# The last product transposed, and for the second pair of batches computed by seven block products instead of eight

## Chip, cores and metric

The kernel runs on one core of a Trainium2 chip. The metric is the device time of one execution in microseconds; the time before is the median of three runs.

## The reference

Attention of tokens against a state gives 4 x (512 + 32) = 2176 rows of 512 numbers; a softplus layer (512 to 2048 to 512) and a gated SiLU layer (512 to 1536 to 512) follow. Cut to what matters here:

```python
x = np.concatenate([xread, sread], axis=2)      # 4 batches, 512 tokens + 32 state rows, 512
h = x @ w_in
g = np.maximum(h, 0.0) + np.log1p(np.exp(-np.abs(h)))
x = g @ w_out                                   # layer one
g = x @ w_gate
silu = g * (1.0 / (1.0 + np.exp(-g)))
val = x @ w_val
out = silu * val @ w_out                        # layer two, its last product
```

## The kernel before

Every float32 operand is split into a high and a low part (fp32r), and every product takes three matmuls: high·high, low·high, high·low (`mm3`, L85 to L89). The split is a copy on ACT (`split_act`, L574) and a subtraction on POOL (`low`, L92).

Layer one (to 350 us) isn't touched. Layer two runs in 24 steps n: pair p = n // 12 of two batches, slice f = n % 12 of 128 hidden columns. In a step gate and value for both batches of the pair are one 2x2 block product, done in Strassen's way by seven products P1 to P7 of six matmuls each (`quad_mm`, `PARTS`), 128x128 stationary and 128x512 moving. P1, P6, P7 and P4 add up in one PSUM bank, px, and between them ACT copies it to cA (L891), cB (L904) and cC (L912); P5 and P3 add up in pz, P2 stands in py. DVE adds py to cA (L901), pz to cC (L918), multiplies px by cA (L922), which is the activation of the pair's first batch (cA), and adds pz to cB (L927). ACT's Silu of cB (L875) and POOL's product with cC (L876) give that of the second batch (cC); the latter, and the split of both, fall into the beginning of the next step.

The last product (`out_mm`) runs two steps later for an f-pair q of two slices: in step n that of slices n-2-n%2 and the next, batch n%2. For each of four row groups r a 128x128 slice of the activation is stationary and w2 (512 columns) moves, six matmuls into a bank po, which DVE adds to oacc in SBUF (L595; for q = 0 a copy, L592). In the rows of the trace w is w2, and h and l are the high and low part of an activation. Two groups stand after P6 and two after P7 in each step (`outs`), 24 matmuls; those of the last f-pair stand at the very end, and at q = 5 each group is stored (L598). The 32 state rows of all batches go through three small products (`state_1` to `state_3`) in steps 0 to 13.

The order of the work is written out by hand: the Python order of the calls is the order on every engine. Small pieces of other work (splitting the second layer's weights into DRAM, the split of the second pair's inputs) are hung on named points of a step by `at2` and run by `run2`. SP issues all DMAs in program order: `load_gw` (L230, four of 512 KB for step n+2 at the end of step n), `load_w2` (L234, two of 512 KB in odd steps), stores.

Of the kernel before, what the change touches and what calls it, by code (L numbers as in the profile page):

```python
# [8 lines left out]
F32 = mybir.dt.float32  # L9
F32R = mybir.dt.float32r  # L10
# [6 lines left out]
P = 128  # L17
# [20 lines left out]
def attention_moe_moe2_kernel(  # L38
# [540 lines left out]
    out_v = out.rearrange("(b t) d -> b t d", b=B)

    def out_mm(n, j, r, store=True):

        p, q = n // NF, n % NF // 2
        b = 2 * p + j
        ps = bank("y", f"po{n}_{j}_{r}")
        t = slice(r * P, (r + 1) * P)
        for f in range(2):
            mm3(ps, [x[:, t] for x in act[n + f, j]], [w2[n + f][:, i, :] for i in range(2)], f == 0, f == 1)
        if q == 0:
            if r % 2 == 0:  # L590
                oacc[b, r // 2] = slot([P, 2, DM], F32, "yacc", f"oacc{b}_{r // 2}")
            nc.vector.tensor_copy(oacc[b, r // 2][:, r % 2, :], ps)  # L592
            return
        v = oacc[b, r // 2][:, r % 2, :]
        nc.vector.tensor_tensor(out=v, in0=ps, in1=v, op=ALU.add)  # L595
# [35 lines left out]
    def state_3(q):  # L631
        ps = bank("y", f"pt3{q}")
        for f in range(2):
            t = slice(f * P, (f + 1) * P)
            mm3(ps, [x[:, t] for x in gs[q]], [w2[2 * q + f][:, i, :] for i in range(2)], f == 0, f == 1)
        if q == 0:
            os_[0] = const.tile([P, DM], F32, tag="yo", name="os_")
            nc.vector.tensor_copy(os_[0], ps)
        else:
            nc.vector.tensor_tensor(out=os_[0], in0=ps, in1=os_[0], op=ALU.add)  # L640
        if q == NQ - 1:
            for b in range(B):
# [8 lines left out]
    with tc.manual_schedule(engines={ENG.PE}):  # L651
# [220 lines left out]
        pending = []  # L872

        def value_times_gate(n, c):
            nc.scalar.activation(c["B"], c["B"], AF.Silu)  # L875
            nc.gpsimd.tensor_tensor(out=c["C"], in0=c["C"], in1=c["B"], op=ALU.mult)  # L876
            yield
            split_act(n, 1, c["C"])

        with tc.manual_schedule(engines={ENG.DVE, ENG.SP, ENG.Activation, ENG.Pool}):  # L880
            run2(-1, "load0")
            run2(-1, "load1")
            for n in range(NS2):
                run2(n, "load0")
                run2(n, "load1")
                c = {}
                for k in "ABC":
                    c[k] = work.tile([P, 512], F32, tag=k, name=f"c{k}{n}")
                x = quad_bank(f"px{n}")
                quad_mm(x, n, "P1", True)  # L890
# [32 lines left out]
                split_act(n, 0, c["A"])  # L923
# [4 lines left out]
                pending.append(value_times_gate(n, c))  # L928
# [49 lines left out]
```

## Time and profile before

| what | value |
|---|---|
| median of 3 runs | 744.88 us (744.71 to 745.37) |
| span of the profiled execution | 742.8 us |
| PE busy | 717.5 us, 97%, 3640 matmuls |
| DVE, POOL, ACT busy | 442.5, 389.6, 316.0 us |
| DMA moved | 143.78 MB, mean 194 GB/s |

The profile gives the profiled execution's own time by its span alone, 742.8 us, from the first to the last recorded work; the runs' times include what lies around it. Busy time is that of one engine; waits and their releasers are inferred from semaphores.

### The profile page before, as it was taken

To read this page: it belongs to the slowest core of one execution; us is meant where nothing else is said; L and a number is where in the kernel's file an instruction comes from. 1 tells how busy PE (TensorE), PEld (TensorE's weight loads), DVE (VectorE), ACT (ScalarE), POOL (GpSimd) and SP (SyncE) were. 2 spreads that over 40 slices of the span, in tenths; PEclk is the share of its full clock that TensorE was granted. 3 is DMA by queue.
4 is the path that set the end of the run, shared out by engine and by line. 5 is a ranking of instruction groups with operands and counts; after the bars stand their busy time and mean duration, and the time that the engine had idled before them with its cause. 6 is when DMAs were issued, how large, how long until landed. Compare 5 with 4: busy or idle time off the path is not lost.

```text
span 742.8 us, 10024 instructions
## 1 busy us (share of the span) xinstructions
PE 717.5 (97%) x3640; PEld 567.3 (76%) x3640; DVE 442.5 (60%) x605; ACT 316.0 (43%) x586; POOL 389.6 (52%) x352
## 2 busy tenths in 40 slices
PE   4699999999999999999999999999999999999997
PEld 1367767786777777788788888888888888888885
DVE  5984559877767867458676656554554333333334
ACT  3767445644545545444544444442542222222221
POOL 2467537787648765834576767765452222222222
PEclk9999999999999999999999999999999999999999
DMA  9930215654544545470579979778355943447302
GB/s 339 408 118 0 86 58 170 197 201 169 160 152 168 192 124 169 160 265 1 197 286 356 348 258 340 286 284 307 114 198 189 315 162 142 170 133 262 143 1 113
DMA packets 51072, 143.78 MB, mean 194 GB/s; under 512 B 5712, under 2 KB 18000, under 8 KB 51024
## 3 DMA queue, kind: packets, MB, share of 16 engines
q1 hardware_dynamic: 51024, 143.15, 54.5%
q8 instruction: 28, 0.46, 0.2%
q14 instruction: 20, 0.16, 0.1%
HBM read 107.22 MB, written 35.91 MB: 193 GB/s over the span
## 4 chain that ended last, share of the span: by engine, by line
PE 86%; DVE 2%; POOL 2%; issue 1%; ACT 1%; DVEq 0%; POOLq 0%; ACTq 0%
PE py L89 25%; PE px L89 18%; PE po L89 18%; PE ph L89 9%; PE pz L89 9%; PE pt L89 3%; PE ps L505 2%; PE pm L374 2%; PE ps L89 1%; POOL sums_gv L193 1%; POOL gv L92 0%; POOL l L92 0%; DVE t_wo L136 0%; DVE m L92 0%; DVE t_win L143 0%
## 5 line engine op out<-in xcount | busy, mean ns | idle before, releaser
L89 PE MATMUL py<-h,wo 128*128 128x512 f32 x512 | 158.8, 391 | 1.5 <-POOL wo L92 1.3
L92 POOL TENSOR_TENSOR l<-C,h 128x512 fp32r<-128x512 f32 x64 | 91.2, 1430 | 86.5 <-ACT C L407 68.9
L89 PE MATMUL po<-w,h 128*128 128x512 f32 x384 | 126.2, 391 | 0.0
L89 PEld LDWEIGHTS py<-h,wo 128*128 128x128 f32 x512 | 95.9, 188 | 23.0 <-POOL wo L92 2.0
L89 PE MATMUL ph<-aT,m 128*128 128x512 f32 x384 | 101.3, 399 | 1.6 <-DVE m L92 1.6
L89 PE MATMUL py<-l,wo 128*128 128x512 f32 x256 | 99.9, 390 | 0.0
L89 PEld LDWEIGHTS ph<-aT,m 128*128 128x128 f32 x384 | 70.8, 188 | 25.5 <-issue 6.1
L404 ACT ACTIVATE h<-ph 128x512 fp32r<-128x512 f32 x64 | 38.2, 597 | 120.6 <-PE py L89 116.7
L595 DVE TENSOR_TENSOR oacc<-po,oacc 128x512 f32<-128x512 f32 x80 | 54.8, 690 | 54.9 <-PE po L89 54.3
L89 PEld LDWEIGHTS po<-w,h 128*128 128x128 f32 x384 | 72.1, 188 | 14.8
L92 POOL TENSOR_TENSOR l<-cC,h 128x512 fp32r<-128x512 f32 x24 | 31.5, 1313 | 97.0 <-ACT h L574 83.1
L89 PE MATMUL po<-w,l 128*128 128x512 f32 x192 | 74.8, 390 | 0.5 <-POOL l L92 0.5
L92 POOL TENSOR_TENSOR l<-cA,h 128x512 fp32r<-128x512 f32 x24 | 34.5, 1438 | 77.6 <-ACT h L574 77.6
L89 PE MATMUL px<-T_0s,gw 128*128 128x512 f32 x216 | 60.9, 390 | 1.4 <-ACT cC L912 1.4
L89 PE MATMUL px<-T_1s,gw 128*128 128x512 f32 x216 | 60.7, 389 | 0.0
L89 PEld LDWEIGHTS py<-l,wo 128*128 128x128 f32 x256 | 48.1, 188 | 10.5 <-POOL l L92 0.3
L574 ACT ACTIVATE h<-cA 128x512 fp32r<-128x512 f32 x24 | 15.2, 633 | 91.9 <-DVE cA L922 91.9
L89 PEld LDWEIGHTS px<-T_0s,gw 128*128 128x128 f32 x216 | 40.3, 188 | 10.3 <-ACT cC L912 2.2
L89 PEld LDWEIGHTS px<-T_1s,gw 128*128 128x128 f32 x216 | 40.5, 188 | 8.5
L89 PEld LDWEIGHTS po<-w,l 128*128 128x128 f32 x192 | 36.1, 188 | 8.2 <-POOL l L92 1.0
L901 DVE TENSOR_TENSOR cA<-py,cA 128x512 f32<-128x512 f32 x24 | 16.5, 687 | 42.6 <-PE py L89 36.9
L92 POOL TENSOR_TENSOR split_gv<-sums_gv,split_gv 128x512 fp32r<-128x512 f32 x24 | 33.1, 1379 | 15.2 <-ACT split_gv L197 14.3
(148 smaller groups left out, 1321.1 us busy)
## 6 DMA issues: line engine op xcount, KB each, us to landing
gw<-gv_d SPq DMA_DIRECT2D x96, 512.0 KB, 6.7
gv_d<-gv SPq DMA_DIRECT2D x24, 512.0 KB, 3.6
gv_d<-split_gv SPq DMA_DIRECT2D x24, 512.0 KB, 3.3
w<-w_d SPq DMA_DIRECT2D x24, 512.0 KB, 8.4
raw_win<-in_moe_w_in_dram SPq DMA_DIRECT2D x16, 512.0 KB, 7.2
raw_wo<-in_moe_w_out_dram SPq DMA_DIRECT2D x16, 512.0 KB, 4.0
raw_gv<-in_moe_w_gate_dram SPq DMA_DIRECT2D x48, 128.0 KB, 3.8
raw_gv<-in_moe_w_val_dram SPq DMA_DIRECT2D x48, 128.0 KB, 3.5
```

Of the source, the lines that this page charges most:

```text
L89: nc.tensor.matmul(o, a[s], b[t], start=first and i == 0, stop=last and i == 2, **k)
L92: eng.tensor_tensor(out=o, in0=whole, in1=high.bitcast(F32), op=ALU.subtract)
L193: nc.gpsimd.tensor_tensor(out=o, in0=x, in1=y, op=op)
L374: nc.tensor.matmul(ps[k * NS:(k + 1) * NS, :], st[q, k, b, :], win[c, k].t[q, :], start=True, stop=True)
L404: nc.scalar.activation(self.h, self.ps, AF.Softplus)
L505: nc.tensor.matmul(ps, sw[:, kt, :], win[c, kt].t, start=kt == 0, stop=kt == KT - 1)
L574: nc.scalar.activation(h, src, AF.Copy)
L595: nc.vector.tensor_tensor(out=v, in0=ps, in1=v, op=ALU.add)
L901: nc.vector.tensor_tensor(out=c["A"], in0=y, in1=c["A"], op=ALU.add)
```

## The change

1. The last product is transposed: a 128x128 slice of w2 is stationary and the activation's 512 tokens move. The token part of the output is kept as [batch, column, token] and turned on the host; the state rows go to a second output. In a group the matmuls now read high, high, low of the activation, where they read high, low, high.
2. For the second pair, f-pairs q = 0 to 4 (steps 14 to 23), the last product of both batches and both slices is a 2x2 block product by seven products of six matmuls (`out_part`) instead of eight groups: parts P1, P2, P5 in the even step, P6, P3, P7, P4 in the odd one. It needs four sums of w2 (`OutSums`, made in steps 10, 12, 13, 14 and 16, kept in DRAM, loaded back by `load_w2s`), four sums of activations (`total`, on DVE) and seven splits instead of four. P1, P6, P7 and P4 use one pair of banks after another, P5 and P3 another.
3. In steps 0 and 1 the order P1, P5, P2, P6, state rows, P7, P4, P3 becomes P1, P5, P6, P2, P7, state rows, P4, P3.
4. In odd steps the out part P4 stands between the products P4 and P3 of the step.

```diff
+    class OutSums:
+        def __init__(self, q):
...
+                t = slot([P, 2, 512], F32R, "made", f"w2r{q}_{f}")
+                nc.sync.dma_start(out=t.bitcast(F32), in_=w2_d[2 * q + f])
+        def whole(self):
...
+                nc.vector.tensor_tensor(out=t, in0=r[:, 0].bitcast(F32), in1=r[:, 1].bitcast(F32), op=ALU.add)
+        def sums(self):
+            (a11, a21), (a12, a22) = ((t[:, :256], t[:, 256:]) for t in self.t)
...
+                nc.gpsimd.tensor_tensor(out=o, in0=x, in1=y, op=op)
+        def high(self):
...
+                nc.scalar.activation(o[:, 0, :], self.s[k], AF.Copy)
+        def low(self):
...
+                low(nc.gpsimd, o[:, 1, :], self.s[k], o[:, 0, :])
+                nc.sync.dma_start(out=w2s_d[self.q][:, k], in_=o.bitcast(F32))
+    def load_w2s(q):
+        for k in range(2):
+            w2s[q, k] = slot([P, 2, 512], F32R, "w2s", f"w2s{q}_{k}")
+            nc.sync.dma_start(out=w2s[q, k].bitcast(F32), in_=w2s_d[q][:, k])
...
-            mm3(ps, [x[:, t] for x in act[n + f, j]], [w2[n + f][:, i, :] for i in range(2)], f == 0, f == 1)
+            mm3(ps, [w2[n + f][:, i, dt * P:(dt + 1) * P] for i in range(2)], act[n + f, j], f == 0, f == 1)
...
+    OUTS = {
+        "P1": ("f0", 0, "B11"), "P2": ("f1", 0, "B21"), "P3": ("s", 3, "B22"), "P4": ("f1", 1, "T4"),
+        "P5": ("s", 0, "T1"), "P6": ("s", 1, "T2"), "P7": ("s", 2, "T3"),
+    }
+    def out_part(n, part):
...
+        keep, opens = ("x", part == "P1") if part in ("P1", "P6", "P7", "P4") else ("z", part in ("P2", "P5"))
...
+            ps = opx[keep, i]
...
+            mm3(ps, [w[:, l, c] for l in range(2)], act[n, t], opens, True, skip_group_check=True)
+            out_add(b + j, 2 * m + i, ps, first)
...
+        SLOTS2 = ((("P1",), ("P2",), ("P5",)), (("P6",), ("P3", "P7"), ("P4",)))
+        for q, n in enumerate((10, 12, 13, 14, 16)):
+            at2(n - 1, "load1", lambda q=q, job=job: job.update(s=OutSums(q)))
+            for kind, name in (("conv0", "whole"), ("conv1", "sums"), ("conv2", "high"), ("conv2", "low")):
...
+                def first():
+                    total(c["B"], c["C"], c["A"], ALU.subtract)
+                    split_act((n, "T1"), c["B"])
...
+                def second():
+                    total(b12, b22, b12, ALU.subtract)
+                    total(b11, b12, b11, ALU.add)
+                    split_act((n - 1, "T2"), b11)
+                    split_act((n - 1, "B22"), b22)
+                def third():
+                    total(b21, b21, b11, ALU.subtract)
+                    split_act((n - 1, "T3"), b12)
+                after(n + 1, 1, second)
+                after(n + 1, 2, third)
+                after(n + 2, 0, lambda: split_act((n - 1, "T4"), b21))
...
                 if n < 2:
+                    quad_mm(x, n, "P6", False)
+                    nc.scalar.activation(c["B"], x, AF.Copy)
+                    quad_mm(y, n, "P2", True)
...
+                    quad_mm(x, n, "P7", False)
+                    nc.scalar.activation(c["C"], x, AF.Copy)
+                    nc.scalar.activation(c["A"], c["A"], AF.Silu)
...
+                    nc.vector.tensor_tensor(out=c["C"], in0=z, in1=c["C"], op=ALU.add)
                     run2(n, "state")
...
-                outs(n, 2)
+                parts(n, 1) if n >= NF + 2 else outs(n, 2)
                 quad_mm(x, n, "P4", False)
...
+                if n >= NF + 2:
+                    parts(n, 2)
...
+                if n % 2 and NF - 1 <= n < NS2 - 3:
+                    load_w2s((n + 1) % NF // 2)
```

On PE, step 0 before, from P2 to P4. Every product has two rows of three matmuls, one for each half of the contraction; B21 is the operand of P2, T2 of P6, T3 of P7 and T4 of P4, and pt holds the state rows:

```order
L89 MATMUL py0_3408<-B21_0_0s_3090,gw0_0_0_3227 128x512 x3
L89 MATMUL py0_3408<-B21_0_1s_3122,gw0_1_0_3229 128x512 x3
L89 MATMUL px0_3393<-T2_0_0s_3265,gw0_0_1_3231 128x512 x3
L89 MATMUL px0_3393<-T2_0_1s_3331,gw0_1_1_3233 128x512 x3
L89 MATMUL pt10_3429<-gw0_0_0_3227,yT_3297 128x256 x3
L89 MATMUL pt10_3429<-gw0_1_0_3229,yT_3297 128x256 x3
L89 MATMUL pt10_3429<-gw0_0_0_3227,yT_3297 128x256 x3
L89 MATMUL pt10_3429<-gw0_1_0_3229,yT_3297 128x256 x3
L89 MATMUL px0_3393<-T3_0_0s_3219,gw0_0_1_3231 128x512 x3
L89 MATMUL px0_3393<-T3_0_1s_3311,gw0_1_1_3233 128x512 x3
L89 MATMUL px0_3393<-T4_0_0s_3309,gw0_0_0_3227 128x512 x3
L89 MATMUL px0_3393<-T4_0_1s_3348,gw0_1_0_3229 128x512 x3
```

And after the change:

```order
L90 MATMUL px0_3393<-T2_0_0s_3265,gw0_0_1_3231 128x512 x3
L90 MATMUL px0_3393<-T2_0_1s_3331,gw0_1_1_3233 128x512 x3
L90 MATMUL py0_3408<-B21_0_0s_3090,gw0_0_0_3227 128x512 x3
L90 MATMUL py0_3408<-B21_0_1s_3122,gw0_1_0_3229 128x512 x3
L90 MATMUL px0_3393<-T3_0_0s_3219,gw0_0_1_3231 128x512 x3
L90 MATMUL px0_3393<-T3_0_1s_3311,gw0_1_1_3233 128x512 x3
L90 MATMUL pt10_3437<-gw0_0_0_3227,yT_3297 128x256 x3
L90 MATMUL pt10_3437<-gw0_1_0_3229,yT_3297 128x256 x3
L90 MATMUL pt10_3437<-gw0_0_0_3227,yT_3297 128x256 x3
L90 MATMUL pt10_3437<-gw0_1_0_3229,yT_3297 128x256 x3
L90 MATMUL px0_3393<-T4_0_0s_3309,gw0_0_0_3227 128x512 x3
L90 MATMUL px0_3393<-T4_0_1s_3348,gw0_1_0_3229 128x512 x3
```

P6 stands before P2, and the four rows of the state (twelve matmuls) have moved from before P7 to between P7 and P4.

On PE, step 17 before, the last eight matmuls of the out product, then P4 and P3 of the step (po14_1_2 and po14_1_3 are row groups 2 and 3 of batch 1; w is w2, h and l the activation's parts):

```order
L89 MATMUL po14_1_2_5881<-w215_5489,l15_1_5771 128x512
L89 MATMUL po14_1_2_5881<-w215_5489,h15_1_5770 128x512
L89 MATMUL po14_1_3_5889<-w214_5487,h14_1_5659 128x512
L89 MATMUL po14_1_3_5889<-w214_5487,l14_1_5660 128x512
L89 MATMUL po14_1_3_5889<-w214_5487,h14_1_5659 128x512
L89 MATMUL po14_1_3_5889<-w215_5489,h15_1_5770 128x512
L89 MATMUL po14_1_3_5889<-w215_5489,l15_1_5771 128x512
L89 MATMUL po14_1_3_5889<-w215_5489,h15_1_5770 128x512
L89 MATMUL px17_5820<-T4_1_0s_5218,gw17_0_0_5699 128x512 x3
L89 MATMUL px17_5820<-T4_1_1s_5221,gw17_1_0_5701 128x512 x3
L89 MATMUL pz17_5830<-B22_1_0s_5231,gw17_0_1_5703 128x512 x3
L89 MATMUL pz17_5830<-B22_1_1s_5234,gw17_1_1_5705 128x512 x3
```

After the change, step 17 from the out part P7 on (poP1_14_0 and poP1_14_1 are the pair of banks that P1 opened in step 16; w2s are loaded sums):

```order
L90 MATMUL poP1_14_0_5874<-h14_T3_5949,w2s1_1_5571 128x512 x2
L90 MATMUL poP1_14_0_5874<-l14_T3_5950,w2s1_1_5571 128x512
L90 MATMUL poP1_14_1_5879<-h14_T3_5949,w2s1_1_5571 128x512 x2
L90 MATMUL poP1_14_1_5879<-l14_T3_5950,w2s1_1_5571 128x512
L90 MATMUL px17_5971<-T4_1_0s_5245,gw17_0_0_5818 128x512 x3
L90 MATMUL px17_5971<-T4_1_1s_5248,gw17_1_0_5820 128x512 x3
L90 MATMUL poP1_14_0_5874<-h14_T4_5979,w215_5567 128x512 x2
L90 MATMUL poP1_14_0_5874<-l14_T4_5980,w215_5567 128x512
L90 MATMUL poP1_14_1_5879<-h14_T4_5979,w215_5567 128x512 x2
L90 MATMUL poP1_14_1_5879<-l14_T4_5980,w215_5567 128x512
L90 MATMUL pz17_5985<-B22_1_0s_5258,gw17_0_1_5822 128x512 x3
L90 MATMUL pz17_5985<-B22_1_1s_5261,gw17_1_1_5824 128x512 x3
```

The groups of six into one bank have become parts of two groups of three, which go on adding in banks that DVE has read before; T4's part stands behind the step's own P4. Step 17 keeps 24 matmuls of this product, the even step 16 has 18.

On SP, from the gw loads at the end of step 13, before:

```order
L230 DMA gw15_1_1_5485<-gv3_d_2015 128x1024
L234 DMA w214_5487<-w22_d_1824 128x1024
L234 DMA w215_5489<-w23_d_2184 128x1024
L230 DMA gw16_0_0_5591<-gv4_d_2222 128x1024
L230 DMA gw16_1_0_5593<-gv4_d_2222 128x1024
L230 DMA gw16_0_1_5595<-gv4_d_2222 128x1024
```

And after:

```order
L233 DMA gw15_1_1_5563<-gv3_d_2015 128x1024
L237 DMA w214_5565<-w22_d_1824 128x1024
L237 DMA w215_5567<-w23_d_2184 128x1024
L281 DMA w2s1_0_5569<-w2s1_d_5370 128x1024
L281 DMA w2s1_1_5571<-w2s1_d_5370 128x1024
L276 DMA w2s3_d_5652<-w2o3_0_5648 128x1024
L276 DMA w2s3_d_5652<-w2o3_1_5649 128x1024
L233 DMA gw16_0_0_5701<-gv4_d_2222 128x1024
L233 DMA gw16_1_0_5703<-gv4_d_2222 128x1024
L233 DMA gw16_0_1_5705<-gv4_d_2222 128x1024
L233 DMA gw16_1_1_5707<-gv4_d_2222 128x1024
```

Behind the loads of w2 stand two loads of sums and two stores of new sums, and gw16 comes after them.

## Rows read from the trace of the kernel before

**Rows 1.** Page, part 1: busy time and share of the span of each engine

```profile
PE 717.5 (97%) x3640; PEld 567.3 (76%) x3640; DVE 442.5 (60%) x605; ACT 316.0 (43%) x586; POOL 389.6 (52%) x352
```

**Rows 2.** Page, part 4: the chain that ended last, by engine

```profile
PE 86%; DVE 2%; POOL 2%; issue 1%; ACT 1%; DVEq 0%; POOLq 0%; ACTq 0%
```

**Rows 3.** Windows, one step: length, busy PE PEld DVE ACT POOL, clock, DMA share, GB/s

```profile
591.00:606.00 15.00, 15.00 (x68) 12.43 (x67) 5.54 (x8) 3.98 (x7) 3.87 (x3) 1.00 0.44 139
```

**Rows 4.** Timeline of PE in steps 13 and 14: start, us, what

```profile
566.38 0.39 PE L89 MATMUL po<-w,h 128*128 128x512 f32 x1
...
569.10 0.39 PE L89 MATMUL px<-T_0s,gw 128*128 128x512 f32 x1
...
577.26 0.84 PE L89 MATMUL px<-B_0s,gw 128*128 128x512 f32 x3
```

**Rows 5.** Waits of PE from 340 us on: us in total, times, longest

```profile
PE px L89 <- ACT cC L912: 1.4, 2, 0.7
PE po L89 <- POOL l L92: 0.5, 1, 0.5
```

**Rows 6.** Timeline of PE in steps 0 and 1

```profile
349.67 0.84 PE L89 MATMUL px<-B_0s,gw 128*128 128x512 f32 x3
...
355.11 1.59 PE L89 MATMUL pt<-gw,yT 128*128 128x256 f32 x12
356.55 0.86 PE L89 MATMUL px<-T_0s,gw 128*128 128x512 f32 x3
...
358.78 0.96 PE L89 MATMUL px<-T_0s,gw 128*128 128x512 f32 x3 [0.69 <-ACT cC L912]
...
361.63 0.84 PE L89 MATMUL px<-B_0s,gw 128*128 128x512 f32 x3
...
373.59 0.84 PE L89 MATMUL px<-B_0s,gw 128*128 128x512 f32 x3
```

**Rows 7.** Timeline of ACT in step 0

```profile
351.29 0.60 ACT L891 ACTIVATE cA<-px 128x512 f32<-128x512 f32 x1 [5.95 <-PE px L89]
...
358.13 0.60 ACT L912 ACTIVATE cC<-px 128x512 f32<-128x512 f32 x1 [0.21 <-PE px L89]
```

**Rows 8.** Timeline of all engines at the end of step 23

```profile
725.04 0.62 PE L89 MATMUL px<-T_1s,gw 128*128 128x512 f32 x2
...
725.70 0.69 DVE L922 TENSOR_TENSOR cA<-px,cA 128x512 f32<-128x512 f32 x1 [0.67 <-PE px L89]
...
727.13 1.29 POOL L92 TENSOR_TENSOR l<-cA,h 128x512 fp32r<-128x512 f32 x1 [3.03 <-ACT h L574]
727.31 0.61 PE L89 MATMUL po<-w,h 128*128 128x512 f32 x2
...
728.47 0.50 PE L89 MATMUL po<-w,l 128*128 128x512 f32 x1 [0.55 <-POOL l L92]
...
728.81 0.62 PE L89 MATMUL po<-w,h 128*128 128x512 f32 x2
```

**Rows 9.** Timeline of DVE and of POOL where both work in SBUF, step 11

```profile
533.67 1.78 DVE L92 TENSOR_TENSOR T_1s<-yacc,T_1s 128x512 fp32r<-128x512 f32 x1
...
534.86 1.75 POOL L92 TENSOR_TENSOR B_1s<-yacc,B_1s 128x512 fp32r<-128x512 f32 x1
```

**Rows 10.** Timeline of SP at gw13's issue; windows with DMA share and GB/s last

```profile
543.86 2.15 SPq L230 DMA_DIRECT2D gw<-gv_d  x4
...
460.00:477.00 17.00, 17.00 (x82) 14.33 (x81) 10.14 (x15) 6.98 (x14) 11.84 (x14) 1.00 0.98 368
480.00:486.00 6.00, 6.00 (x28) 4.96 (x27) 3.10 (x5) 1.72 (x4) 4.54 (x7) 1.00 0.82 242
500.00:505.00 5.00, 5.00 (x30) 4.37 (x29) 1.38 (x2) 2.24 (x5) 4.62 (x5) 1.00 0.97 297
543.90:605.80 61.90, 61.90 (x275) 51.24 (x274) 25.83 (x36) 18.29 (x33) 18.65 (x14) 1.00 0.68 228
576.00:591.00 15.00, 15.00 (x68) 12.43 (x67) 5.54 (x8) 3.98 (x7) 3.87 (x3) 1.00 0.95 317
```

More of the change, by code (lines that the diff above doesn't have):

```diff
@@ L224, in attention_moe_moe2_kernel @@
     w2 = {}
+    w2s = {}
+    w2s_d = {}
     def load_gw(n):
@@ L578, in attention_moe_moe2_kernel @@
     oacc = {}
[L579 to L586, printed above, removed]
-        for f in range(2):
-            mm3(ps, [x[:, t] for x in act[n + f, j]], [w2[n + f][:, i, :] for i in range(2)], f == 0, f == 1)
[L589 to L595, printed above, removed]
-        if q == NQ - 1:
-            o = out_v[b, :S, :].rearrange("(p r) d -> p r d", r=R)
-            nc.sync.dma_start(out=o[:, r, :], in_=v)
+    out_v = out_st.rearrange("(b t) d -> b t d", b=B)
@@ new lines, in out_add, with out_store, out_mm @@
+    def out_add(b, dt, ps, first):
+        if (b, dt // 2) not in oacc:
+            oacc[b, dt // 2] = slot([P, 2, 512], F32, "yacc", f"oacc{b}_{dt // 2}")
+        v = oacc[b, dt // 2][:, dt % 2, :]
+        if first:
+            nc.vector.tensor_copy(v, ps)
+        else:
+            nc.vector.tensor_tensor(out=v, in0=ps, in1=v, op=ALU.add)
+    def out_store(b, dt):
+        nc.sync.dma_start(out=out[b, dt * P:(dt + 1) * P, :], in_=oacc[b, dt // 2][:, dt % 2, :])
+    def out_mm(n, j, dt):
+        q = n % NF // 2
+        b = 2 * (n // NF) + j
+        ps = bank("y", f"po{n}_{j}_{dt}")
+        for f in range(2):
+            mm3(ps, [w2[n + f][:, i, dt * P:(dt + 1) * P] for i in range(2)], act[n + f, j], f == 0, f == 1)
+        out_add(b, dt, ps, q == 0)
+        if q == NQ - 1:
+            out_store(b, dt)
@@ new lines, in attention_moe_moe2_kernel @@
+    OUTS = {
+        "P1": ("f0", 0, "B11"), "P2": ("f1", 0, "B21"), "P3": ("s", 3, "B22"), "P4": ("f1", 1, "T4"),
+        "P5": ("s", 0, "T1"), "P6": ("s", 1, "T2"), "P7": ("s", 2, "T3"),
+    }
+    opx = {}
+    def out_part(n, part):
+        q = n % NF // 2
+        kind, k, t = OUTS[part]
+        b = 2 * (n // NF)
+        keep, opens = ("x", part == "P1") if part in ("P1", "P6", "P7", "P4") else ("z", part in ("P2", "P5"))
+        j, m = {"P1": (0, 0), "P2": (0, 0), "P5": (1, 1), "P6": (1, 0), "P3": (1, 0), "P7": (1, 1), "P4": (0, 1)}[part]
+        first = q == 0 and part in ("P1", "P5", "P6", "P4")
+        last = q == NQ - 1 and part in ("P2", "P3", "P7", "P4")
+        for i in range(2):
+            if opens:
+                opx[keep, i] = bank("y", f"po{part}_{n}_{i}")
+            ps = opx[keep, i]
+            c = slice(k % 2 * 256 + i * P, k % 2 * 256 + (i + 1) * P)
+            w = w2s[q, k // 2] if kind == "s" else w2[n + int(kind[1])]
+            mm3(ps, [w[:, l, c] for l in range(2)], act[n, t], opens, True, skip_group_check=True)
+            out_add(b + j, 2 * m + i, ps, first)
+            if last:
+                out_store(b + j, 2 * m + i)
@@ L869, in outs, with parts @@
                     out_mm(n - 2 - n % 2, n % 2, r)
-        pending = []
-        def value_times_gate(n, c):
[L875 to L878, printed above, removed]
+        SLOTS2 = ((("P1",), ("P2",), ("P5",)), (("P6",), ("P3", "P7"), ("P4",)))
+        def parts(n, k):
+            for part in SLOTS2[n % 2][k]:
+                out_part(n - 2 - n % 2, part)
@@ new lines, in attention_moe_moe2_kernel, with after, run_later @@
+        for q, n in enumerate((10, 12, 13, 14, 16)):
+            job = {}
+            at2(n - 1, "load1", lambda q=q, job=job: job.update(s=OutSums(q)))
+            for kind, name in (("conv0", "whole"), ("conv1", "sums"), ("conv2", "high"), ("conv2", "low")):
+                at2(n, kind, lambda name=name, job=job: getattr(job["s"], name)())
+        whole = {}
+        later = {}
+        def after(n, point, fn):
+            later.setdefault((n, point), []).append(fn)
+        def run_later(n, point):
+            for fn in later.pop((n, point), ()):
+                fn()
@@ new lines, in total, with times @@
+        def total(o, x, y, op):
+            nc.vector.tensor_tensor(out=o, in0=x, in1=y, op=op)
+        def value_times_gate(n, c):
+            def times():
+                nc.scalar.activation(c["B"], c["B"], AF.Silu)
+                nc.gpsimd.tensor_tensor(out=c["C"], in0=c["C"], in1=c["B"], op=ALU.mult)
+            after(n + 1, 0, times)
+            if n < NF or n >= NS2 - 2:
+                after(n + 1, 1, lambda: split_act((n, 1), c["C"]))
+            elif n % 2 == 0:
+                def first():
+                    total(c["B"], c["C"], c["A"], ALU.subtract)
+                    split_act((n, "T1"), c["B"])
+                    whole["B11"], whole["B12"] = c["A"], c["C"]
+                after(n + 1, 1, first)
+            else:
+                b11, b12, b21, b22 = whole["B11"], whole["B12"], c["A"], c["C"]
+                def second():
[9 more added lines that the diff above has]
+                after(n + 2, 0, lambda: split_act((n - 1, "T4"), b21))
@@ L891, in attention_moe_moe2_kernel @@
                 nc.scalar.activation(c["A"], x, AF.Copy)
-                for part in pending:
-                    next(part)
+                run_later(n, 0)
                 run2(n, "P1")
```

92 lines of the change are left out of this document (60 added, 32 removed).

## Prediction

> **What bounds the kernel now.** I read the busy shares first. PE is busy 717.5 of 742.8 us, the other engines 60% and less [rows 1], and the chain of work that ended last lies on PE for 86% of the span [rows 2]. So an edit pays by what it takes off PE's queue or out of PE's waits, and costs only where it makes PE wait. Then the windows by step, since a share over the span mixes stages: a step of the second pair of batches lasts 15.00 us, with PE busy in all of it at a granted clock of 1.00, DVE 5.54, ACT 3.98 and POOL 3.87 us [rows 3]. Nothing but PE has to be beaten there.
>
> The price of a matmul comes from the start times, not from the 390 ns durations, which overlap: twelve matmuls of the out product issue from 566.38 to 569.10 us [rows 4], 0.2267 us each. 42 + 24 of them are 14.96 us, the 15.00 of the window.
>
> The list of PE's waits shows what is lost beside that from 340 us on: two waits of a layer-two product on cC and one of the out product on l [rows 5]. Both are in places that the change touches.
>
> **The change, part by part.**
>
> *Seven products for eight.* For f-pairs q = 0 to 4 of the second pair, 48 matmuls of 128x512 become 42. That is 5 x 6 = 30 fewer, the shape stays 128x512 and so does the pace: 30 x 0.2267 = **6.80 us**. An even step falls from 66 to 60 matmuls (15.0 to 13.6 us), an odd one stays at 66. The Trainium skill, "TensorE: Matmul & The Clock Gate", section "Back-to-back issue gap", gives about 131 ns as the sustained spacing of N=512 matmuls with their weight loads; by it the 30 would be worth 3.9 us (an estimate), and the time would come out near 738.6. The trace disagrees: 227 ns with the same weight loads [rows 4].
>
> *Transposition.* The out product has as many matmuls with as many weight loads as before; only operands change sides. Both are 128-row slices, so I count nothing. The order high, high, low puts the read of the low activation third instead of second in a group. Stores carry the same bytes; the transposition back is on the host.
>
> *Steps 0 and 1.* From the first P1 to the next step's P1 it is 361.63 - 349.67 = 11.96 us, and 11.96 again for step 1 [rows 6]. The work in it is 42 x 0.2267 = 9.52 and the state rows' 12 half-width matmuls from 355.11 to 356.55, 1.44; together 10.96. So 1.00 us is lost per step, where P4 waits for the copy cC of P7's bank (the waits' column shows 0.69 of it, since modelled ends overlap). P7 begins at 356.55, so its last matmul issues at 356.55 + 5 x 0.2267 = 357.68; cC starts at 358.13 and P4 at 358.78 [rows 6, 7], 1.10 us after that issue. In the new order the state rows stand between P7 and P4: P4 comes at the earliest 0.23 + 1.44 = 1.67 us after it, so this wait is covered with 0.57 to spare. Late next is P6, which now has only P5's six matmuls between itself and P1: P1's last matmul issues at 349.67 + 5 x 0.2267 = 350.80, the copy cA is there at 351.29 + 0.60 = 351.89 [rows 7], P6 comes at 349.67 + 12 x 0.2267 = 352.39, a margin of 0.50. In step 1 ACT has another copy of some 0.6 us that can stand in front of it, and P3 needs DVE's addition cC, which stands behind weight work on DVE. So of the 2.00 I take **1.6**; the ends are 0 and 2.0.
>
> *The tail.* P4's last matmul of step 23 issues at 725.04 + 0.23 = 725.27; DVE makes cA at 725.70, and POOL ends its low part at 727.13 + 1.29 = 728.42. PE wanted it at 727.31 + 2 x 0.2267 = 727.77, went on at 728.47 and took 0.34 for the next matmul: 0.70 + 0.11 = 0.81 lost [rows 8]. After the change six matmuls of the out part P4, the six of P3 and five of the group stand before the first reader of l: 725.27 + 18 x 0.2267 = 729.35, 0.9 after it is ready. I take **0.8**, with 0 as the other end.
>
> *Work added at no cost.* Per two steps (28.6 us) DVE gets six more evictions and four sums, at 0.69 each 6.9 us: 11.1 + 6.9 = 18.0, 63%. ACT gets three copies, POOL three low parts at 1.29: 7.7 + 3.9 = 11.6, 41%. What covers them is PE itself: all run beside matmuls. The sums of w2 (five jobs, steps 10 to 16) add for each two DVE sums, six POOL operations of at most 1.29 us (7.7 us at most), two ACT copies. The tight places are new waits inside a chain: parts P1, P6, P7, P4 use one pair of banks, each after DVE evicted the one before. Worst is the odd step: P7's two groups end after P3's, the quad product P4 (6 matmuls, 1.36 us) lies between, and DVE must do cC and four evictions at some 0.6 us each from the end of the quad P7. They end 4.0 us after it, the second P4 group wants its bank at 18 + 3 matmuls, 4.76 us: a slack of 0.5 to 0.8 us. If that cover is gone, each microsecond of lateness is one of PE's, five times. DVE sums queue behind matmul evictions, so a late one delays POOL's split and then a part a step later, with 1 us or more of margin.
>
> *DMAs.* Per job: two reads of w2, two stores of sums, two loads of them, 0.524 MB each. They share SP's queue with the gw loads, in order. From gw13's first issue (543.86 [rows 10]) to the start of step 16 (step 14's 577.26 [rows 4] + 13.6 + 15.0 = 605.9) 61.9 us are there. In SP's order up to gw16's last load stand 16 gw (8.39 MB), 4 w2 (2.10), 4 loads of sums (2.10), 4 reads (2.10), 6 stores of sums (3.15), the output (2.36): 20.2 MB, 326 GB/s, where this stretch moved 228 [rows 10]. With the engines nearly full, rows show 317 GB/s at a share of 0.95 and 368 at 0.98, that is 334 to 375 at 1: 54 to 60.5 us, so it fits by 1.4 to 8 us, and I count nothing. At the lower 297 at 0.97 (306) it would take 66.0 us, 4.1 late.
>
> The sum: 6.80 + 1.6 + 0.8 = **9.2**; the span goes from 742.8 to 733.6. The median of the runs lies 744.88 - 742.8 = 2.1 above the profiled span (launch and end, unchanged): **735.7 us**.
>
> **Rivals.**
>
> *Loads fall behind.* For it: 326 GB/s are wanted for 62 us, and the stretch of 297 shows that full engines can give less. Against it: small pieces of raw weights, which were moving then, are gone by step 12, and the window 576 to 591 ran at a share of 0.95 without a wait of PE. A stall of up to 4 us in steps 15 and 16 gives up to 739.8; chance 0.11. The same mechanism ends on the other side where the supply falls to 20.2 MB / (61.9 + 9.2) = 284 GB/s; at the 242 of the slowest row [rows 10] 83.5 us are needed, 21.6 late, some 2 of it harmless since the last load of a set is used later in the step: 19.6, so 755. That row has a share of 0.82, it was not full; chance 0.04.
>
> *Odd steps stall on DVE.* Where DVE and POOL work on two tensors in SBUF at once, a DVE sum took 1.78 us and a POOL low part 1.75 [rows 9], against 0.69 and 1.29 alone. The added sums are such operations; one of them 1.1 us longer eats the 0.5 to 0.8 us of slack and leaves 0.3 to 0.6 in each of five odd steps: 1.5 to 3 us, 737.2 to 738.7. The Trainium skill's "GPSIMD Engine Reference", section "1. Specifications", says that POOL shares its SBUF interfaces with VectorE and suffers from DVE instructions with two SBUF inputs; [rows 9] agree. Against it: in most of the step the two don't meet. Chance 0.15.
>
> *The two waits only move.* P6 behind cA, or P3 behind DVE in steps 0 and 1, and the tail's l behind something else: only the 6.8 remain, 738.1. Chance 0.07. That the 30 are not gone is excluded by the instruction order.
>
> *A removed matmul is worth less than its spacing.* If weight loads, not matmuls, set the pace, a pair is worth a load: PEld is busy 12.43 us for the 66 of a step [rows 3], 0.188 each, 30 of them 5.6 us, so 736.9; chance 0.01, since PE and not PEld is busy throughout.
>
> **How the numbers follow.** The forecast, 735.7, has 0.62, with a range of its own from 735.3 (all of 2.0 and 0.81) to 736.5. Below: 734.5 leaves room for the pace and the spread of runs. Above: 739.5 takes in the moved waits, the odd steps and nearly all of the late loads, and leaves out about 0.1. A measurement of this kernel can tell about 0.2%, 1.5 us, from no change: faster means below 743.4. All cases but the slow loads are there: faster 0.94, same 0.02, slower 0.04.
>
> **What would show it.** Right: steps of 13.6 and 15.0 us in turn from step 14 on, no wait of PE in steps 0 and 1 of 0.3 us or more, steps 0 and 1 near 11.0 to 11.2 us, no wait of po on l at the end. Wrong: waits of a po part on DVE's evictions in odd steps; of px in steps 14 to 16 on a DMA; PE waits for cA in step 1. The prediction falls if the DMA share stands at 1 from 545 to 605 us with PE idle.

## The result, and the profile after

| | before | changed | difference |
|---|---|---|---|
| median of 4 runs, us | 745.12 | 736.99 (736.69 to 738.44) | -8.13 |
| ratio, 95% interval | | 0.9896 [0.9882, 0.9910] | -8.8 to -6.7 us |
| span of the profiled execution | 742.8 | 735.4 | -7.4 |
| first matmul of step 0 to the last matmul | 388.69 | 380.96 | -7.73 |

735.7 was forecast, in a range from 734.5 to 739.5: the time lies in it, 1.3 us above the forecast, and 0.5 us above the 735.3 to 736.5 that the forecast had as its own range. The gain of 9.2 us came out as 8.1.

The last line of the table is the one to work with. Layer one has the same instructions in the same order on PE in all kernels below, and yet step 0 began anywhere from 348.33 to 351.30 us in the thirteen profiles. Counting from step 0 on takes that scatter out; the 8.13 and the 7.73 differ by less than it.

The page of the changed kernel, parts 1 and 4, beside [rows 1, 2]:

```profile
PE 710.3 (97%) x3610; PEld 561.7 (76%) x3610; DVE 488.1 (66%) x665; ACT 329.0 (45%) x611; POOL 441.7 (60%) x397
...
PE 82%; POOL 3%; issue 2%; ACT 2%; DMA 2%; DVE 1%; SPq 0%; DVEq 0%; ACTq 0%; POOLq 0%
```

Thirty matmuls are gone, DVE has 45.6 us more to do and POOL 52.1, and still the chain is PE's. DMA has come into the chain with 2%.

The starts of the steps are read from PE's timeline (start, duration, tiles, wait in brackets), beside [rows 4, 6]:

```profile
349.87 0.84 PE L90 MATMUL px<-B_0s,gw 128*128 128x512 f32 x3
...
360.85 0.84 PE L90 MATMUL px<-B_0s,gw 128*128 128x512 f32 x3
...
371.14 0.96 PE L90 MATMUL pz<-B_0s,gw 128*128 128x512 f32 x3 [0.48 <-DVE cC L1039]
...
372.63 0.84 PE L90 MATMUL px<-B_0s,gw 128*128 128x512 f32 x3
...
389.26 0.84 PE L90 MATMUL px<-B_0s,gw 128*128 128x512 f32 x3
...
398.36 0.97 PE L90 MATMUL px<-T_0s,gw 128*128 128x512 f32 x3 [0.78 <-ACT cB L1047]
...
408.12 0.84 PE L90 MATMUL px<-B_0s,gw 128*128 128x512 f32 x3
...
577.38 0.84 PE L90 MATMUL px<-B_0s,gw 128*128 128x512 f32 x3
...
590.98 0.84 PE L90 MATMUL px<-B_0s,gw 128*128 128x512 f32 x3
...
605.94 0.84 PE L90 MATMUL px<-B_0s,gw 128*128 128x512 f32 x3
...
705.22 0.84 PE L90 MATMUL px<-B_0s,gw 128*128 128x512 f32 x3
...
730.83 0.39 PE L90 MATMUL po<-l,w 128*128 128x512 f32 x1
```

From one step's first row to the next, in us (before: step 23 from 711.90 to the last matmul at 738.36; steps 4 to 13 are alike within 0.02 in both; the rows of before that neither [rows 4] nor [rows 6] shows come first):

```profile
390.22 0.84 PE L89 MATMUL px<-B_0s,gw 128*128 128x512 f32 x3
...
408.00 0.84 PE L89 MATMUL px<-B_0s,gw 128*128 128x512 f32 x3
...
711.90 0.84 PE L89 MATMUL px<-B_0s,gw 128*128 128x512 f32 x3
...
738.36 0.39 PE L89 MATMUL po<-w,h 128*128 128x512 f32 x1
```

| step | 0 | 1 | 2 | 3 | 14, 16 .. 22 | 15, 17 .. 21 | 23 to the last matmul |
|---|---|---|---|---|---|---|---|
| before | 11.96 | 11.96 | 16.63 | 17.78 | 14.96 | 14.96 | 26.46 |
| changed | 10.98 | 11.78 | 16.63 | 18.86 | 13.60 | 14.96 | 25.61 |
| difference | -0.98 | -0.18 | 0 | **+1.08** | 5 x -1.36 | 0 | -0.85 |

The differences add up to the 7.73. The second half came as it was worked out: -6.80 for the thirty matmuls, to the hundredth, and -0.85 for the tail (0.8 forecast). The first half is the surprise: steps 0 and 1 won 1.16 and step 3, in which the change only turns the last product, gave 1.08 back. The list of PE's waits from 340 us on says the same, beside [rows 5]:

```profile
PE px L90 <- ACT cB L1047: 0.8, 1, 0.8
PE pz L90 <- DVE cC L1039: 0.5, 1, 0.5
```

The windows (length, busy PE, PEld, DVE, ACT, POOL, clock, DMA share, GB/s) of step 15 and of the stretch in which the loads pile up, beside [rows 3, 10]:

```profile
591.00:606.00 15.00, 15.00 (x68) 12.43 (x67) 8.89 (x14) 4.51 (x8) 9.10 (x7) 1.00 1.00 347
...
544.00:606.00 62.00, 62.00 (x276) 51.30 (x275) 39.66 (x54) 23.84 (x43) 40.22 (x36) 1.00 0.97 349
```

The DMA engines are nearly full for 62 us (a share of 0.97), at 349 GB/s against the 326 that I had counted, and PE waits for none of it. What makes P7 wait in step 3 is in the timelines of ACT and SP, first of the changed kernel, then of the one before:

```profile
396.64 0.63 ACT L153 ACTIVATE w<-t_w 128x512 fp32r<-128x512 f32 x1 [4.71 <-DMA gv_d<-gv]
...
397.73 0.58 ACT L1047 ACTIVATE cB<-px 128x512 f32<-128x512 f32 x1
```
```profile
379.62 0.32 SPq L200 DMA_DIRECT2D gv_d<-split_gv  x1
380.03 2.23 SPq L233 DMA_DIRECT2D gw<-gv_d  x4
...
392.99 0.85 SPq L182 DMA_DIRECT2D gv_d<-gv  x2
```
```profile
395.34 0.63 ACT L152 ACTIVATE w<-t_w 128x512 fp32r<-128x512 f32 x1 [2.44 <-DMA gv_d<-gv]
...
396.43 0.59 ACT L904 ACTIVATE cB<-px 128x512 f32<-128x512 f32 x1
```
```profile
378.94 2.22 SPq L230 DMA_DIRECT2D gw<-gv_d  x4
```

ACT stands 4.71 us before a weight copy that wants a slot of three in SBUF, until a store of the tile that held it has landed; the copy cB, which PE waits for, is behind it in ACT's queue. That store was issued at 392.99, behind loads that SP could only begin at 380.03, since a store ahead of them waited for POOL until 379.62. In the kernel before those loads began at 378.94 and the copy at 395.34; there the same copy waited too, 2.44 us, but PE began P7 only at 398.38, 1.95 us after cB began, where 0.63 is enough (398.36 less 397.73). So 1.3 us were to spare, and they went at both ends: counted from step 0, PE wants P7 1.16 us earlier and the weight copy comes 1.1 us later. (Of the second part some may be chance: in e1 below, with the old order, the copy came 0.7 us later than before.)

### The profile page after: what moved, and what is told of

The parts are those of the page before. It is cut to its first block, busy times and chain, and to the rows that moved or that the text cites. A ratio compares the mean times of both kernels' runs of the same rounds, so it can differ in the third digit from the quotient of the medians.

```text
span 735.4 us, 10173 instructions
## 1 busy us (share of the span) xinstructions
PE 710.3 (97%) x3610; PEld 561.7 (76%) x3610; DVE 488.1 (66%) x665; ACT 329.0 (45%) x611; POOL 441.7 (60%) x397
## 4 chain that ended last, share of the span: by engine, by line
PE 82%; POOL 3%; issue 2%; ACT 2%; DMA 2%; DVE 1%; SPq 0%; DVEq 0%; ACTq 0%; POOLq 0%
PE py L90 25%; PE px L90 16%; PE ph L90 10%; PE po L90 9%; PE pz L90 8%; PE poP L90 6%; PE pt L90 3%; PE ps L552 2%; PE pm L421 2%; PE ps L90 1%; DMA gv_d<-gv 1%; POOL l L93 1%; DMA raw_gv<-in_moe_w_gate_dram 1%; POOL gv L93 1%; POOL sums_gv L194 1%
## 5 line engine op out<-in xcount | busy, mean ns | idle before, releaser
L93 POOL TENSOR_TENSOR l<-C,h 128x512 fp32r<-128x512 f32 x64 | 94.1, 1476 | 78.7 <-PE py L90 51.6
L90 PE MATMUL po<-h,w 128*128 128x512 f32 x224 | 69.6, 392 | 0.0
L90 PEld LDWEIGHTS po<-h,w 128*128 128x128 f32 x224 | 41.6, 188 | 8.4
L635 DVE TENSOR_TENSOR oacc<-po,oacc 128x512 f32<-128x512 f32 x48 | 32.4, 687 | 22.9 <-PE po L90 22.8
L635 DVE TENSOR_TENSOR oacc<-poP,oacc 128x512 f32<-128x512 f32 x62 | 40.7, 686 | 10.3 <-PE poP L90 10.3
L93 POOL TENSOR_TENSOR l<-cA,h 128x512 fp32r<-128x512 f32 x14 | 21.4, 1528 | 38.2 <-ACT h L621 38.2
L90 PE MATMUL po<-l,w 128*128 128x512 f32 x112 | 43.6, 390 | 0.0
L500 DVE TENSOR_TENSOR yacc<-py,yacc 128x512 f32<-128x512 f32 x48 | 31.3, 685 | 16.7 <-PE py L90 16.7
L93 POOL TENSOR_TENSOR gv<-t_gv,gv 128x512 fp32r<-128x512 f32 x24 | 33.4, 1393 | 14.2 <-issue 11.7
L137 DVE TENSOR_SCALAR t_gv<-t_gv 128x512 int32<-128x512 int32 x24 | 22.1, 920 | 28.2 <-ACT t_gv L133 28.1
```

Of the source, the lines that this page charges most:

```text
L93: eng.tensor_tensor(out=o, in0=whole, in1=high.bitcast(F32), op=ALU.subtract)
L137: nc.vector.tensor_scalar(out=ti, in0=ti, scalar1=3, scalar2=0x7FFFFFF8, op0=ALU.logical_shift_left, op1=ALU.bitwise_and,)
L500: nc.vector.tensor_tensor(out=v, in0=yps[dt], in1=v, op=ALU.add)
```

## Experiments

Two theories of the step that gave the gain back. A: the preparation of layer two's weights on POOL, SP and the DMAs sets the pace of steps 0 to 3, and whatever PE wins there it waits for later; A1 puts that on the order in the queues, A2 on POOL's own work. B: the wait in step 3 has nothing to do with the new order. Ratios are to runs of the kernel before on the same chip (medians 744.47 to 745.12). "Steps 0 to 3" and "from step 0" (to the last matmul) are read from each profile as above; without any wait steps 0 to 3 would take 10.98 + 10.98 + 16.63 + 17.78 = 56.37.

| kernel | steps 0 to 3 | from step 0 | median, ratio |
|---|---|---|---|
| before | 58.33 | 388.69 | 745.12 |
| changed | 58.25 | 380.96 | 736.99, 0.9896 [0.9882, 0.9910] |
| e1 old order | 58.33 | 381.04 | 736.73, 0.9896 [0.9881, 0.9911] |
| e2 eight groups | 58.40 | 388.61 | 743.93, 0.9993 [0.9984, 1.0002] |
| e3 ACT first | 57.95 | 381.59 | 736.16, 0.9890 [0.9876, 0.9903] |
| e4 DVE first | 58.20 | 380.96 | 736.42, 0.9895 [0.9881, 0.9908] |
| f1 loads first | 58.07 | 380.79 | 735.88, 0.9882 [0.9869, 0.9896] |
| f2 less POOL | 57.40 | 380.59 | 735.46, 0.9876 [0.9861, 0.9891] |
| f3 P4 early | 58.15 | 385.58 | 741.44, 0.9961 [0.9949, 0.9974] |
| f4 more loads | 58.10 | 383.52 | 740.79, 0.9948 [0.9936, 0.9961] |
| g1 in order | 56.76 | 379.47 | 734.46, 0.9861 [0.9848, 0.9875] |
| g2 low on DVE | 58.64 | 381.35 | 735.87, 0.9882 [0.9868, 0.9895] |
| g3 low alone | 59.12 | 381.83 | 738.51, 0.9920 [0.9906, 0.9933] |

**e1: steps 0 and 1 in the old order.**

```diff
-                if n < 2:
-                    quad_mm(x, n, "P6", False)
...
-                else:
+                if True:
...
+                    if n < 2:
+                        run2(n, "state")
                     quad_mm(x, n, "P7", False)
```

> The changed kernel with steps 0 and 1 in their old order. Theory A (the weight preparation on POOL, SP and the DMAs sets the pace of steps 0 to 3, so what the new order wins in steps 0 and 1 is given back in step 3): steps 0 and 1 take 11.96 us each again (+1.16), the wait of P7 in step 3 goes (18.86 to 17.78, -1.08), in all +0.1: 737.1. Theory B (the wait in step 3 has nothing to do with the order): it stays, +1.16: 738.1.

Steps 0 and 1 took 11.97 and 11.95 again, step 3 17.78, and the time stayed. Of PE's waits only the two on cC in steps 0 and 1 are left, as in [rows 5]:

```profile
PE px L90 <- ACT cC L1039: 1.4, 2, 0.7
```

A holds and B falls: the new order by itself is worth nothing here.

**e2: no block product, no sums of w2.**

```diff
-                    parts(n, 0) if n >= NF + 2 else outs(n, 0)
+                    outs(n, 0)
...
-                parts(n, 1) if n >= NF + 2 else outs(n, 2)
+                outs(n, 2)
```

> The changed kernel with the transposed last product, but eight groups of six for the second pair and no sums of w2. If a removed matmul is worth its spacing: steps 14 to 23 take 14.96 us each, +6.8; at the end l is read by the 6th matmul after P3 where the old kernel read it with the 5th and six matmuls fewer lie before it than in the changed one, so 0.58 of the old 0.81 comes back: in all +7.4, 744.4. If a matmul is worth 131 ns: +3.9 and the tail, 741.5. If the tail's gain came from the order high, high, low alone: +6.8, 743.8.

All steps from 14 to 22 took 14.96, and the tail 26.31, 0.70 more than in the changed kernel, with the wait on l back:

```profile
PE po L90 <- POOL l L93: 0.4, 1, 0.4
```

+7.65 from step 0 on: a removed matmul was worth its spacing of 0.2267. The 131 ns of the Trainium skill ("TensorE: Matmul & The Clock Gate", "Back-to-back issue gap"), by which +3.9 (an estimate) and the tail would have come, are not what this kernel shows. The transposition with the new order alone is no gain over before (0.08 us, ratio 0.9993).

**e3: in step 3 ACT's weight work behind the copy cB.**

```diff
-                    run2(n, "conv0")
+                    if n != 3:
+                        run2(n, "conv0")
...
                     nc.scalar.activation(c["A"], c["A"], AF.Silu)
+                    if n == 3:
+                        run2(n, "conv0")
```

> The changed kernel, in step 3 alone the weight work of its first point behind the copy cB of P6's bank on ACT. If ACT's queue, held by a weight copy that waits for a slot, is what P7 waits for: step 3 takes 17.78 instead of 18.86, -1.08: 735.9. If the late weights are needed there in any case: the wait shows up at another product of steps 3 to 6, 737.0.

Step 3 took 17.78. In this profile step 1, ahead of the edit, lost 0.77 more (1.26 of wait on cC), so that PE reached step 3 later, and by theory A that alone would shrink its wait. The rows part the two: the weight copy now stands behind cB and comes at 396.81, and P7 begins at 397.62. From that copy to P7 the changed kernel took 1.72 us (396.64 to 398.36), so ahead of cB the copy would have held P7 until some 398.5.

```profile
396.81 0.63 ACT L153 ACTIVATE w<-t_w 128x512 fp32r<-128x512 f32 x1 [0.59 <-DMA gv_d<-gv]
```
```profile
397.62 0.84 PE L90 MATMUL px<-T_0s,gw 128*128 128x512 f32 x3
```

So ACT's queue is what P7 waited for. Step 5 lost 0.41 and step 14 0.51 behind the edit; from step 0 on it is 0.63 slower, by the medians 0.8 faster. Its time settles nothing; its step 3 does.

**e4: DVE's cC ahead of its weight work.**

```diff
                     nc.scalar.activation(c["A"], c["A"], AF.Silu)
+                    nc.vector.tensor_tensor(out=c["C"], in0=z, in1=c["C"], op=ALU.add)
                     run2(n, "conv1")
                     run_later(n, 1)
                     run2(n, "P7")
-                    nc.vector.tensor_tensor(out=c["C"], in0=z, in1=c["C"], op=ALU.add)
```

> The changed kernel, in steps 0 and 1 DVE's addition cC ahead of its weight work. Both theories: step 1 takes 10.98 instead of 11.78, -0.8. Theory A: the weights become no earlier, so step 3's wait grows by as much, 19.6, in all 0: 737.0. Theory B: step 3 stays at 18.86, in all -0.8: 736.2.

Step 1 took 11.29, step 2 17.52 and step 3 18.41: the wait moved from P3 in step 1 to P6 in step 2, and the sum from step 0 on is the same to the hundredth.

```profile
PE px L90 <- ACT cA L1018: 0.6, 1, 0.6
PE px L90 <- ACT cB L1047: 0.3, 1, 0.3
```

A as expected, though I had put all of it into step 3.

**f1: loads ahead of the waiting stores in step 1.** Stores of step 1's last two weight points are held back until its loads are issued:

```diff
+    def put_d(out, in_):
+        if holding[0]:
+            held.append((out, in_))
+        else:
+            nc.sync.dma_start(out=out, in_=in_)
...
+                holding[0] = n == 1
                 run2(n, "conv2")
```

> The changed kernel; in step 1 the two stores of weights that wait for POOL (at 376.9 and 379.6) are issued behind the loads of gw3 and w2, not ahead of them. Theory A1 (SP's queue, held by POOL, leaves the DMAs idle from 374 to 380, and the burst behind it delays the store that frees ACT's slot in step 3): gw3 is issued at 373, the wait of P7 in step 3 goes, 18.86 to 17.78, in all -1.1: 735.7 (steps 0 to 3: 57.2). Theory A2 (POOL's own pace): the wait stays, 58.2 for steps 0 to 3, 736.7.

The loads were issued at 371.16, and the window from 372.6 to 380, first of the changed kernel and then of this one, shows the DMAs filled:

```profile
372.60:380.00 7.40, 7.40 (x34) 6.12 (x33) 4.99 (x7) 4.69 (x8) 7.40 (x8) 1.00 0.49 197
```
```profile
372.60:380.00 7.40, 6.86 (x30) 5.32 (x29) 3.12 (x6) 4.02 (x8) 7.40 (x7) 1.00 1.00 345
```

Step 3 took 17.78, and the weight copy that had come at 396.64 was there at 391.81 without a wait, so its wait was indeed SP's queue:

```profile
391.81 0.62 ACT L153 ACTIVATE w<-t_w 128x512 fp32r<-128x512 f32 x1
```

But an earlier store now landed late, in the stretch that the loads fill, and ACT's next weight copy waits for that slot in step 2, with the copy cA behind it (0.88 lost):

```profile
375.34 0.63 ACT L207 ACTIVATE split_gv<-sums_gv 128x512 fp32r<-128x512 f32 x1 [2.66 <-DMA gv_d<-gv]
375.88 0.58 ACT L1027 ACTIVATE cA<-px 128x512 f32<-128x512 f32 x1
```

The same mechanism one step earlier; A1 is half right.

**f2: less work for POOL.** It leaves out the sums of two weight pieces, so the layer-two weights of two slices are not the reference's:

```diff
                 for name in names:
+                    if name == "sums" and t < 8:
+                        made_short.append(j)
+                        continue
```

> The changed kernel without the sums of two weight pieces on POOL in steps 0 and 1 (eight operations of 0.46 us; those pieces' second half is split from the weights in place of their sums, so the layer-two weights of two slices are not the reference's). Theory A2 (POOL's pace is behind all of it): POOL is 1.9 us ahead from step 1 on and 3.7 from step 2, the wait of P7 in step 3 goes, -1.1: 735.7. Theory A1: the store of step 1 comes 2 us earlier too and so do the loads, so the wait goes as well; both fall if it stays at 0.8. If POOL and SP have nothing to do with the wait of P3 in step 1, that stays at 0.4 to 1.3.

Step 2 16.65, step 3 18.02: 0.84 of the 1.08 came back, and the wait of P3 in step 1 stayed (0.5). It does not part A1 from A2, as a quicker POOL frees SP's queue too. Its step 14 took 14.08, much as e3's 14.11; of that below.

**f3: the out part P4 ahead of the product P4.**

```diff
-        SLOTS2 = ((("P1",), ("P2",), ("P5",)), (("P6",), ("P3", "P7"), ("P4",)))
+        SLOTS2 = ((("P1",), ("P2",), ("P5",)), (("P6",), ("P3", "P7", "P4"), ()))
```

> The changed kernel with the out part P4 right behind P7, ahead of the step's product P4. By the prediction's slack: its first group wants the bank 2.72 us after the quad P7, DVE has evicted it at 3.3 to 3.4, so 0.6 us is lost in each of the odd steps 15 to 23, 3.0 in all; and at the end six matmuls fewer lie ahead of l: 0.4 to 0.6. In all +3.5: 740.3. If DVE's evictions are quicker than I count: +0.5 at most, 737.3.

PE's waits and, of step 15, DVE's four evictions and the matmul behind them:

```profile
PE poP L90 <- DVE oacc L635: 2.5, 5, 0.5
...
PE po L90 <- POOL l L93: 0.3, 1, 0.3
```
```profile
601.04 2.48 DVE L635 TENSOR_TENSOR oacc<-poP,oacc 128x512 f32<-128x512 f32 x4
```
```profile
602.97 0.73 PE L90 MATMUL poP<-h_T,w 128*128 128x512 f32 x2 [0.55 <-DVE oacc L635]
```

The odd steps 15 to 21 took 15.75 to 15.80 and the tail 1.45 more: 4.6 us in all from step 0 on, where I expected 3.5. The column shows 0.5 per wait, the steps lose 0.8: what I had read off [rows 6] for the waits on cC holds here too. So the change's place for this part, behind six other matmuls (1.36 us), leaves some 0.5 to 0.65 us (1.36 less what the steps lose, or less the 0.71 by which 602.97 is late), inside my 0.5 to 0.8.

**f4: 2.1 MB more on SP's queue.**

```diff
+                if q in (2, 3):
+                    e = slot([P, 2, 512], F32R, "extra", f"extra{q}_{f}")
+                    nc.sync.dma_start(out=e.bitcast(F32), in_=w2_d[2 * q + f])
```

> The changed kernel with the four reads of w2 for the sums of steps 13 and 14 done twice: 2.1 MB more on SP's queue ahead of gw14 and gw15, 6.0 us at the 349 GB/s that the stretch moved. Last load of gw16 lands some 3 us before step 16 wants it, so PE waits 2 to 4 us at the beginning of steps 15 to 17: +3, 739.8. If the loads have the slack that a share of 326 to 375 GB/s gave (8 us): no wait, 736.8.

```profile
PE px L90 <- DMA gw<-gv_d: 1.1, 1, 1.1
PE pz L90 <- DMA gw<-gv_d: 0.6, 2, 0.4
```

Step 15 took 17.63, 2.67 more, where the loads of gw15 were late. SP issued them at 584.42 in place of 578.10, 6.3 us later. The 2.1 MB alone don't explain that: the extra reads share one buffer, and SP stood before the second until 559.84, with the DMAs at a share of 0.83 from 559.8 to 565 (1.00 in the changed kernel). Rows of the changed kernel, then of f4:

```profile
578.10 2.64 SPq L233 DMA_DIRECT2D gw<-gv_d  x4
```
```profile
593.02 0.84 PE L90 MATMUL pz<-T_1s,gw 128*128 128x512 f32 x3
```
```profile
559.84 0.32 SPq L251 DMA_DIRECT2D extra<-w_d  x1
...
584.42 3.35 SPq L233 DMA_DIRECT2D gw<-gv_d  x4
```

So the loads of gw15 have some 6.3 - 2.7 = 3.6 us to spare in the changed kernel. Its own trace says much the same: the last load of gw15 lands at 588.70 and is read from 593.02 on, that of gw16 at 604.14 and from 607.98 on, 4.3 and 3.8 us. The rival of late loads was some 4 us away, not 8.

**g1, g2, g3: take the waits out.** g1 is e4 and f1 together, and the weight work of step 1's last point moved behind the copy cA of step 2; g2 adds, and g3 does alone, the low part of cA on DVE in steps 0 and 1.

```diff
+                if n == 2:
+                    run2(1, "conv3")
...
-                run2(n, "conv3")
+                if n != 1:
+                    run2(n, "conv3")
```
```diff
-        low(nc.gpsimd, l, src, h)
+        low(nc.vector if key in ((0, 0), (1, 0)) else nc.gpsimd, l, src, h)
```

> The changed kernel with all three waits of steps 1 to 3 taken out by order alone: DVE's cC ahead of its weight work in steps 0 and 1, step 1's store of w2 behind the loads of gw3, and the weight work at the end of step 1 behind the copy cA of step 2. If the order on the queues is what is left (A1): steps 0 to 3 take 10.98, 10.98, 16.63 and 17.78, 56.4 together, 1.9 less than in the changed kernel: 734.9. If POOL's pace sets it (A2): some wait comes back, 57.4 to 58.2, 736 to 736.7.

> As the run before, and in steps 0 and 1 the low part of cA is made by DVE, not POOL (1.74 us less for POOL in each). A2: with POOL 3.5 us ahead the waits go, 56.4 to 56.8: 734.9 to 735.3. A1: as the run before. If DVE is filled by it (8.1 of 12 us busy there): P3 waits for cC in step 1 again, 0.5 to 1.

> The changed kernel, in steps 0 and 1 the low part of cA made by DVE, the order as it was. A2: step 3's wait shrinks from 1.08 to 0 to 0.3, step 1's stays: 57.2 to 57.5 for steps 0 to 3, 736.0. A1: the stores of step 1 come 1.7 us earlier as well, so the same; DVE's wait in step 1 may grow by 0.7.

g1 took 10.98, 11.24, 16.76 and 17.78 for its first four steps, its list of PE's waits from 340 us on is empty, and at 734.46 us it is the fastest kernel of the study, 1.49 us below the changed one from step 0 on:

```profile
349.09 0.84 PE L90 MATMUL px<-B_0s,gw 128*128 128x512 f32 x3
...
405.85 0.84 PE L90 MATMUL px<-B_0s,gw 128*128 128x512 f32 x3
```

The interval of its ratio [0.9848, 0.9875] does not touch the changed kernel's [0.9882, 0.9910], each against its own runs of the kernel before. With POOL's work as it was in amount, order alone brought the steps to 0.39 us of the value without waits: POOL's pace is not the bound, A2 falls, and the gain of some 1.6 that I had forecast for steps 0 and 1 is there once the weight work stands out of its way.

g2 and g3 missed: both are slower than without their edit, by 1.88 and 0.87 us from step 0 on. In g3's step 1 DVE waits for ACT's copy h, and its weight work, cB and ACT's copy cA come behind it:

```profile
364.37 0.95 DVE L93 TENSOR_TENSOR l<-cA,h 128x512 fp32r<-128x512 f32 x1 [0.70 <-ACT h L621]
```
```profile
365.42 0.60 ACT L1018 ACTIVATE cA<-px 128x512 f32<-128x512 f32 x1 [1.08 <-DVE l L93]
```

P6 waited 0.9 for that copy; step 1 took 12.62 and step 2, with a wait of P7 on cB that I did not follow up, 17.74. An operation is not only its duration, it is also the wait that it brings into the queue that it joins.

## Why the prediction was right, and where it missed

The forecast case itself missed by a little: 737.0 lies between its own range (to 736.5) and the rival that only the 6.8 remain (738.1). The wide range would also have held with nothing of the 1.6 for steps 0 and 1 (737.3), so that the time lies in it says nothing for that term. Of the signs of being right the steps of 13.6 and 15.0 and the end without a wait came; those for steps 0 and 1 failed in step 1 (a wait of 0.48, 11.78 us). None of the signs of being wrong came.

*Seven products for eight:* 6.80 forecast, 5 x 1.36 = 6.80 measured, and lost again without the edit (e2).

*The tail:* 0.8 forecast, 0.85 measured; 0.70 comes back in e2, where the part P4 no longer stands ahead.

*Steps 0 and 1:* this is the step that failed. "So of the 2.00 I take 1.6" was 1.16 in place, since P3 did wait for DVE's cC in step 1 (0.8 with its aftermath; a place that I had named, but priced together with ACT's extra copy at 0.4), and 0.08 in the sum, since step 3 gave 1.08 back. That is 1.5 of the 9.2. I had checked PE against the engines that feed it within the step, and not the engines' other work, the weights of steps 2 and on, which did not become ready any earlier when PE did. The wait of P3 in step 1 is in my rival "the two waits only move"; the larger loss, P7 in step 3 behind ACT's weight copy, is in no rival of mine, and the half of that rival that concerns the tail did not happen.

*Work added at no cost:* right. No wait of PE on a po part or on its evictions in the changed kernel, with 0.5 to 0.65 us of slack (f3). The rival on DVE and POOL showed in a small size in two other kernels and in an even step: in the profiles of e3 and f2, step 14 lost 0.5, with the two sums on DVE and a POOL sum prolonged together (rows of e3, DVE, then POOL; the changed kernel had 0.68, 0.69 and 0.74):

```profile
584.52 1.22 DVE L973 TENSOR_TENSOR cC<-cC,cC 128x512 f32<-128x512 f32 x1
585.78 1.11 DVE L973 TENSOR_TENSOR cA<-cC,cA 128x512 f32<-128x512 f32 x1
```
```profile
579.20 1.30 POOL L93 TENSOR_TENSOR w2o<-w2u,w2o 128x512 fp32r<-128x512 f32 x1 [5.09 <-DMA out_dram<-os__3900]
...
585.16 1.18 POOL L265 TENSOR_TENSOR w2u<-w2t,w2u 128x256 f32<-128x256 f32 x1
```

The Trainium skill says that the two engines share SBUF interfaces ("GPSIMD Engine Reference", "1. Specifications"), and these rows agree. Neither edit touches step 14: whether the two meet depends on where POOL's queue happens to stand. In e3 POOL had stood 5.09 us before a split, which in the changed kernel ran at 573.22 to 575.78 without a wait, and its sums ran 1.6 us later, 582.96 to 586.34 against 581.37 to 584.32.

*DMAs:* right. 1.4 to 8 us were counted, some 4 are there (f4), with 349 GB/s at a share of 0.97, which is 360 at 1, in the middle of the 334 to 375.

## What to carry to other kernels

In this kernel a gain for the bounding engine counted only as far as the work that prepares its next stage kept up: look one or two steps beyond the edit, for queues in which a copy that waits for a slot stands ahead of one that the engine needs. Here, moving the waiting instruction behind the needed one was worth 1.5 us (g1), and moving work to another engine made it worse (g2, g3). And where single profiles scatter before the edited place, measure from the first instruction behind the scatter.

## What was not expected of the hardware

With one and the same order of instructions in layer one, the first matmul of step 0 came between 348.33 and 351.30 us over thirteen profiles; what moves it was not looked into. And a matmul stream takes more than its wait to come back: behind the wait of 0.78 the first group of three began at 398.36 and the next 0.80 later instead of 0.68. That 0.12 is part of how 0.5 in the waits' column became 0.8 of a step in f3; the other 0.16 is that the column counts from the modelled end of the matmul before (a matmul that issues 0.71 late shows a wait of 0.55).
